# Splitting the first PSUM copy by bank and moving one softmax piece forward in a fused dynamic convolution and feed-forward kernel

## Chip, cores and metric

Each run is one core of one Trainium2 chip. The metric is the device time of one execution in microseconds (us). Ratios are the mean time of one kernel's runs over the mean of the other's runs of the same rounds, so they are not quite the ratios of the medians that are quoted. Executions over 1.5% slower than the fastest of the same kernel are left out of the means. The 95% intervals belong to the ratios.

## The reference

```python
# dynamic convolution: B=8, S=4096, D=192, H=8 heads, K=7 taps
w = exp(weight_gen - max(weight_gen, -1)); w = w / (sum(w, -1) + 1e-9)
x_pad = concat([zeros(B, 6, D), x], axis=1)
out = einsum('bshk,bskhg->bshg', w, unfold(x_pad))    # 7 rows back, per head
# feed-forward: d_ff = 2048
h = maximum(out.reshape(32768, 192) @ w_in, 0)
return (h * h) @ w_out
```

## The kernel before

TensorE does the convolution as matmuls against banded weights (tile `yp` in PSUM), the first feed-forward matmul (`h`) and the second (`o`). ScalarE evacuates `yp` to `y`, makes `t = relu(h)`, the softmax's exp and half of the output evacuation. VectorE squares (`g = t*t`), sums, inverts and scales the softmax (`ssum`, `rcp`, `v`), makes the bands (`bd`) and adds the second half of the output (`o_sb`). A plan of letters orders the work: `u` is a hidden unit (12 matmuls of 256 columns in the first two blocks, 6 of 512 later, then one `t` and one `g`), `M` half of a pair of second matmul groups, `C` the next block's convolution, `E` an exp, `S` a softmax scaling, `B` the bands.

```python
ps_h = tile_pool(bufs=3, PSUM)        # [128, 1024] f32: two banks a tile; h and yp share it
ps_o = tile_pool(bufs=1, PSUM)        # o0, o1: one bank each
...
def st_conv(j):
    th = n * TB // 2                  # 256 columns in blocks 0 and 1, 512 later
    per = 1024 // th                  # chunks of y in one yp tile: 4, later 2
    yps = [ps_h.tile([P, 2 * TB], f32, name="yp") for _ in range(-(-NK // per))]
    ...                               # matmuls into yps
    for n, yp in enumerate(yps):
        k0, k1 = n * per, min((n + 1) * per, NK)          # NK = 3 chunks
        copies = ((k0, k1, nc.scalar.copy),)
        if j == 0:
            copies = ((0, 1, nc.scalar.copy),) + tuple(
                (k, k + 1, nc.vector.tensor_copy) for k in range(1, NK))
        for a, b, copy in copies:
            copy(out=y[:, a:b, 0:th], in_=yp[:, (a - k0) * th : (b - k0) * th] ...)
...
def soft(s):                          # "S": one piece of a part, all on VectorE
    lo, hi = next(s.softs)
    s.total(lo, hi); s.recip(lo, hi); s.scale(lo, hi, nc.vector)
...
steady = "MuMuuu" * 3 + "MuuuMCu"     # blocks from 4 on; E, S and B are filled in by TIMES
3: "L5 L6 M S3 u u u M u u u u M u M B6 E4 u u u M M B7 u u u M u M C S4 u",
TIMES = {(1, 0): ((3, 15), (4, 1)), ...}     # fifth part: scaled before unit 15 of block 3
                                             # and before unit 1 of block 4
```

The softmax here doesn't subtract the row's maximum and nothing guards it: scores larger than these inputs give would overflow.

## Time and profile before

| | before |
|---|---|
| time, median of the first three runs | 748.18 us (747.88 to 750.02) |
| span of the profiled run, granted clock | 746.1 us, 1.000 |
| TensorE busy | 738.3 us (99%) |
| ScalarE, VectorE busy | 624.1 us (84%), 621.9 us (83%) |

TensorE's busy share of 99% says little of its waits: by the page's own legend, matmuls are pipelined and their ends are modelled. The page says where TensorE is *not* the bound: a chain of work that leaves TensorE, and a wait that it has for another engine. There are two such places, the first 25 us and the head of block 4; the prediction shows their lines.

### The profile page before, as it was taken

The page shows a single profiled execution, that of the slowest core. Times are in us where ns is not written, and L with a number is a line of the kernel's source. Part 1 is how long each engine was busy: PE and PEld are TensorE (multiplying, and loading weights), DVE is VectorE, ACT ScalarE, POOL GpSimd, SP SyncE. Part 2 cuts the span into 40 slices and gives each one's busy share as a digit, 9 for nine tenths or more (in the row PEclk, how much of TensorE's full clock was granted, in tenths as well). Part 3 has the DMA queues.
Part 4 walks back from the last instruction along what each step waited for, and adds up shares of the span by engine and source line. Part 5 has one row for each costly group of instructions (what it writes and reads, how often), then busy time and mean ns, then how long its engine had stood idle before and what let it go on. Part 6 is the DMA issues. An engine that isn't in the chain of part 4 may idle for free.

```text
span 746.1 us, 33290 instructions
## 1 busy us (share of the span) xinstructions
PE 738.3 (99%) x15106; PEld 558.0 (75%) x15106; DVE 621.9 (83%) x1003; ACT 624.1 (84%) x755; POOL 88.9 (12%) x130
## 2 busy tenths in 40 slices
PE   8999999999999999999999999999999999999998
PEld 4767777777777797777877777787777777777787
DVE  5999898998889888887889888898888987677853
ACT  5998888898888888888888888888888888888884
POOL 7322220101101100011000110001100011000000
PEclk9999999999999999999999999999999999999999
DMA  8755444435554244643146442265341354442312
GB/s 218 118 100 115 80 93 93 99 71 139 94 118 80 72 59 80 140 83 71 39 78 139 98 69 61 43 139 108 59 80 47 58 108 80 60 73 51 51 45 66
DMA packets 122170, 64.81 MB, mean 87 GB/s; under 512 B 83850, under 2 KB 118637, under 8 KB 121517
## 3 DMA queue, kind: packets, MB, share of 16 engines
q1 hardware_dynamic: 77708, 45.66, 22.3%
q0 software_dynamic: 44176, 16.93, 20.1%
q8 instruction: 118, 1.93, 1.0%
q14 instruction: 24, 0.19, 0.1%
q10 hardware_dynamic: 144, 0.10, 0.0%
HBM read 48.61 MB, written 28.70 MB: 104 GB/s over the span
## 4 chain that ended last, share of the span: by engine, by line
PE 94%; DVE 3%; DMA 1%; ACT 1%; issue 1%; DVEq 0%; ACTq 0%
PE o L482 45%; PE h L448 43%; PE yp L416 6%; DVE bd L348 1%; DVE g L460 1%; DMA wr<-v_first 0%; DMA wg<-in_weight_gen_dram 0%; ACT t L457 0%; DVE v_first L239 0%; DVE ssum L224 0%; DVE rcp L231 0%; ACT ex L217 0%; DVE o_sb L498 0%; ACT y L434 0%; ACT o_sb L496 0%
## 5 line engine op out<-in xcount | busy, mean ns | idle before, releaser
L457 ACT ACTIVATE t<-h 128x1024 f16<-128x1024 f32 x512 | 496.7, 1026 | 64.8 <-PE h L448 64.4
L460 DVE TENSOR_TENSOR g<-t 128x1024 f16<-128x1024 f16 x512 | 333.9, 686 | 99.6 <-ACT t L457 97.0
L482 PEld LDWEIGHTS <-g 64*128 64x128 f16 (+1 forms) x8032 | 351.5, 94 | 55.0 <-issue 4.1
L482 PE MATMUL o<-w_o,g 64*128 64x192 f16 (+1 forms) x8032 | 383.9, 243 | 0.5 <-DVE o_sb L498 0.5
L448 PE MATMUL h<-y,w_i 64*128 64x512 f16 (+1 forms) x3168 | 378.7, 370 | 1.7 <-ACT t L457 0.8
L448 PEld LDWEIGHTS <-w_i 64*128 64x128 f16 x3168 | 163.5, 94 | 114.8 <-issue 5.0
L348 DVE TENSOR_TENSOR bd<-wr,mask 128x4160 f16<-128x4160 f16 (+3 forms) x89 | 149.3, 1701 | 3.7 <-DMA wr<-v_first 3.7
L300 POOL DMA_DIRECT2D xt<-in_x_dram x62 | 51.6, 836 | 443.0 <-PE yp L416 420.1
L496 ACT COPY o_sb<-o 128x384 f32<-128x384 f32 x129 | 62.3, 483 | 33.9 <-PE o L482 33.9
L498 DVE TENSOR_TENSOR o_sb<-o,o_sb 128x384 f32<-128x384 f32 x123 | 68.2, 554 | 8.4 <-ACT o_sb L496 5.6
L434 ACT CAST y<-yp 128x1024 f16<-128x1024 f32 (+1 forms) x64 | 47.7, 796 | 15.0 <-PE yp L416 15.0
L416 PE MATMUL yp<-bd,xt 128*32 128x104 f16 (+8 forms) x3864 | 51.8, 208 | 0.6 <-DVE bd L348 0.3
L416 PEld LDWEIGHTS <-xt 128*32 128x32 f16 (+3 forms) x3864 | 46.1, 91 | 7.0 <-issue 6.4
L217 ACT ACTIVATE ex<-wg 128x448 f32<-128x448 f32 (+2 forms) x44 | 27.2, 618 | 1.9 <-DMA wg<-in_weight_gen_dram 1.9
L239 DVE TENSOR_TENSOR v_big<-ex,rcp 128x112 f16<-128x112 f32 (+1 forms) x136 | 27.3, 263 | 1.6 <-DMA vd<-v_big 0.4
L224 DVE TENSOR_REDUCE ssum<-ex 128x64 f32<-128x448 f32 (+2 forms) x44 | 26.1, 593 | 2.4 <-ACT ex L217 2.4
L231 DVE RECIPROCAL rcp<-ssum 128x64 f32<-128x64 f32 (+2 forms) x44 | 23.7, 539 | 1.5
L290 POOL DMA_DIRECT2D xt<-in_x_dram x7 | 3.8, 548 | 137.2 <-PE yp L416 137.2
L330 POOL DMA_DIRECT2D wr<-v_first x31 | 16.8, 559 | 18.3 <-DVE v_first L239 18.1
L546 PE MATMUL wp<-warm 128*128 128x512 f16 x39 | 10.5, 434 | 1.3 <-DVE warm L538 1.3
L546 PEld LDWEIGHTS <-warm 128*128 128x128 f16 x39 | 4.2, 110 | 6.9 <-issue 2.4
L239 DVE TENSOR_TENSOR v_first<-ex,rcp 128x112 f16<-128x112 f32 (+1 forms) x48 | 9.1, 255 | 0.3
(25 smaller groups left out, 28.6 us busy)
## 6 DMA issues: line engine op xcount, KB each, us to landing
out_dram<-o_sb SPq DMA_DIRECT2D x63, 384.0 KB, 2.9
xt<-in_x_dram POOLq DMA_DIRECT2D x42, 240.0 KB, 5.7
wg<-in_weight_gen_dram SPq DMA_DIRECT2D x4, 1064.0 KB, 8.2
xt<-in_x_dram POOLq DMA_DIRECT2D x20, 192.0 KB, 5.4
wr<-vd SPq DMA_DIRECT2D x38, 80.0 KB, 3.7
vd<-v_big SPq DMA_DIRECT2D x5, 512.0 KB, 5.5
wg<-in_weight_gen_dram SPq DMA_DIRECT2D x5, 392.0 KB
wg<-in_weight_gen_dram SPq DMA_DIRECT2D x3, 616.0 KB, 4.5
```

Source lines behind the costliest of these rows:

```text
L217: nc.scalar.activation(out=self.ex[:, lo:hi].rearrange("p r g k e -> p (r g) k e"), in_=self.wg[:, lo:hi].rearrange("p r (g e) k -> p (r g ...
L239: eng.tensor_tensor(out=bass.AP(tensor=v.tensor, offset=v.offset + lo * H * SL + lo % SL * 2 + g * SL * 2, ap=[list(v.ap[0]), [H * SL + 2, ...
L300: eng.dma_start(out=dst[:, first:last], in_=ap)
L348: nc.vector.tensor_tensor(out=bd_t[j][:, H * lo : H * (lo + len(tiles) * n)].rearrange("p (g m c) -> p g m c", g=shape[1], c=2 * SL), in0= ...
L416: nc.tensor.matmul(out=yps[k // per][p0 : p0 + m, col + a : col + b], lhsT=x_t[s][:, i, 32 * q : 32 * q + m], rhs=bd[:, h // 2, h % 2, a - ...
L434: copy(out=y[:, a:b, 0:th], in_=yp[:, (a - k0) * th : (b - k0) * th].rearrange("p (k c) -> p k c", c=th),)
L448: nc.tensor.matmul(out=h[:, half, jj * th : (jj + 1) * th], lhsT=w_in_chunk(u * per + jj, slot, half), rhs=y_t[j][r0 : r0 + RT, k, 0:th], ...
L457: nc.scalar.activation(out=t1, in_=h, func=ActF.Relu)
L460: nc.vector.tensor_tensor(out=g, in0=t1, in1=t1, op=AluOp.mult)
L482: nc.tensor.matmul(out=oo[:, cc * Dm : (cc + 1) * Dm], lhsT=g[r0 : r0 + n, cc * P : (cc + 1) * P], rhs=w_o[r0 : r0 + n, fc, :], start=(fc ...
L496: nc.scalar.copy(out=o_sb, in_=o[0][:, c])
L498: nc.vector.tensor_tensor(out=o_sb, in0=o[1][:, c], in1=o_sb, op=AluOp.add)
```

## The change

Its intent has two parts. In block 0 three chunks of y are copied out of PSUM before the first hidden matmuls can run in full. Chunks 0 and 1 fill one bank and chunk 2 lies in the next; each engine is to copy one bank, side by side. In block 4 VectorE has two softmax pieces close together ahead of an output addition that TensorE waits for; one of them goes earlier, into idle time, and its exp goes earlier still.

```diff
             if j == 0:
-                copies = ((0, 1, nc.scalar.copy),) + tuple(
-                    (k, k + 1, nc.vector.tensor_copy) for k in range(1, NK)
-                )
+                copies = ((0, 2, nc.scalar.copy), (2, NK, nc.vector.tensor_copy))
@@
-            3: "... M M B7 u u u M u M C S4 u",
+            3: "... M M B7 u u u E4 M u M C S4 u",
@@
-            (1, 0): ((3, 15), (4, 1)),
+            (1, 0): ((3, 15), (4, 0)),
```

## The prediction

> **What bounds the kernel now.** I read the page first, then the table of waits, then the chain of waits in order of time, and last the timelines of the two stretches that the diff touches. The page:
>
> ```profile
> span 746.1 us, 33290 instructions
> PE 738.3 (99%) x15106; PEld 558.0 (75%) x15106; DVE 621.9 (83%) x1003; ACT 624.1 (84%) x755; POOL 88.9 (12%) x130
> PE 94%; DVE 3%; DMA 1%; ACT 1%; issue 1%; DVEq 0%; ACTq 0%
> ...
> L482 PE MATMUL o<-w_o,g 64*128 64x192 f16 (+1 forms) x8032 | 383.9, 243 | 0.5 <-DVE o_sb L498 0.5
> ```
>
> TensorE is busy for 99% of the span and is 94% of the chain that ended last. From 90 to 732 us the table of busy times by stretch gives it 641.90 of 642.00 us, from 25 to 81 us 55.94 of 56.00. A change outside TensorE can therefore gain only where TensorE stands still. The granted clock is 1.000 and there is one core, so no slow die enters. TensorE stands still in two places that matter here: the start, up to about 25 us, and once in the middle, the single wait for the second output addition (0.5 us) in the last line above. The diff touches exactly these two.
>
> The chain at the first y (start, length, what):
>
> ```profile
> 14.63 0.45 PE yp L416 x16
> 15.09 0.02 issue
> 15.11 0.38 ACT y L434
> ...
> 15.86 0.41 DVE y L434
> 16.27 2.27 DVE bd L348 x2
> ```
>
> and the timeline of 14.9 to 20 us:
>
> ```profile
> 15.11 0.37 ACT L434 CAST y<-yp 128x256 f16<-128x256 f32 x1 [1.94 <-PE yp L416]
> 15.51 0.75 DVE L434 CAST y<-yp 128x256 f16<-128x256 f32 x2 [0.93 <-ACT y L434]
> ...
> 15.99 2.91 PE L448 MATMUL h<-y,w_i 64*128 64x256 f16 x47 [0.19 <-DVE y L434]
> ...
> 16.32 2.29 PEld L448 LDWEIGHTS <-w_i 64*128 64x128 f16 x43 [0.22 <-issue]
> 16.97 2.85 ACT L457 ACTIVATE t<-h 128x1024 f16<-128x1024 f32 x3 [1.49 <-PE h L448]
> ```
>
> The reader is to see that VectorE's copies start only at 15.51, when ScalarE's copy is over, although yp was whole at 15.09. The third chunk is ready at 16.27, and the weight loads pause until 16.32. ScalarE's first squaring input, t, follows at 16.97, and from there to 25 us ScalarE is never idle (5.00 of 5.00 us busy from 20 to 25), so this start sets everything up to 25 us.
>
> The second place, VectorE and then TensorE around the head of block 4:
>
> ```profile
> 79.57 0.69 DVE L460 TENSOR_TENSOR g<-t 128x1024 f16<-128x1024 f16 x1 [0.49 <-ACT t L457]
> 81.34 0.69 DVE L460 TENSOR_TENSOR g<-t 128x1024 f16<-128x1024 f16 x1 [1.08 <-ACT t L457]
> 82.11 0.56 DVE L498 TENSOR_TENSOR o_sb<-o,o_sb 128x384 f32<-128x384 f32 x1
> 82.58 0.49 DVE L224 TENSOR_REDUCE ssum<-ex 128x48 f32<-128x336 f32 x1
> ...
> 86.89 1.89 DVE L460 TENSOR_TENSOR g<-t 128x1024 f16<-128x1024 f16 x3
> 88.69 0.55 DVE L498 TENSOR_TENSOR o_sb<-o,o_sb 128x384 f32<-128x384 f32 x1
> ```
>
> ```profile
> 88.57 0.24 PE L482 MATMUL o<-w_o,g 64*128 64x192 f16 x1
> 89.29 1.48 PE L482 MATMUL o<-w_o,g 64*128 64x192 f16 x31 [0.48 <-DVE o_sb L498]
> ```
>
> VectorE has 1.08 us free before 81.34, and then two softmax pieces (the fifth part's second, 82.58 to 84.23, and a piece of the seventh, 84.83 to 86.89) pile up behind 82.11. The addition that empties the output bank ends at 89.24, and TensorE's second matmul into it waits until 89.29.
>
> **What the Trainium skill says.** The page "PSUM — Partial Sum Buffer", Terms, says that a bank is 2 KiB per partition and that two engines must not be on one bank at once, reads included; its Specifications say that ScalarE and VectorE may read in parallel where there is no bank collision. In block 0 a chunk of yp is 256 fp32 columns, so chunks 0 and 1 fill a bank and chunk 2 lies in the next. That agrees with the trace: VectorE's copy of chunk 1 waited 0.93 us for ScalarE's of chunk 0. No run so far shows the two engines reading different banks of one tile together.
>
> "VectorE: DVE Perf Modes", the errata section, gives copies out of PSUM 120 cycles plus the columns at 0.96 GHz on VectorE and 172 plus the columns at 1.2 GHz on ScalarE: for 256 columns 392 and 357 ns. The trace has 418 and 372, for 512 columns on ScalarE 592 (31 copies; 570 by the page). I use the trace's. "ScalarE: Activation LUTs", section on what a table load costs, says that back-to-back activations overlap by about 93 ns: three t in 2.85 us against 1.026 each are a pitch of 0.91, so 0.11 here.
>
> **Part 1, the first y.** Removed: ScalarE's copy of 256 columns (0.372) and one of VectorE's two (0.418). Added: a ScalarE copy of 512 columns (0.592). VectorE keeps chunk 2 alone, on another bank.
> - ScalarE: 15.11 + 0.59 = 15.70, so chunks 0 and 1 come at 15.70 instead of 15.49 and 15.94.
> - VectorE: chunk 2 from about 15.11 to 15.53, instead of 16.27.
> - TensorE: the first hidden matmul goes at 15.74 (0.04 after its release, as now 15.49 to 15.53). It is 0.2 later, but nothing interrupts it: 47 matmuls in 2.91 us are about 0.06 each, and the fifth, the first that needs chunk 2, goes at 15.74 + 4 x 0.06 = 15.98 instead of 16.32. From that fifth to the first t is 16.97 - 16.32 = 0.65, so t starts at 16.63: **0.34 earlier**.
> - VectorE reaches the bands of the second sub-block at about 15.5 instead of 16.19 (their rows landed by 15.0, and the x tile whose landing released GpSimd's gate at 14.56) and the cast of x at 17.8 instead of 18.45, which opens the second convolution before TensorE gets to it. This 0.7 us lies beside ScalarE's chain and is not added.
> - The next thing that ScalarE can meet is the second part's exp, now at 19.70. Its input's last packet landed at 19.09; at 19.70 - 0.34 = 19.36 it is there, with 0.27 to spare. So the shift should reach 25 us, where TensorE becomes the bound (the chain leaves ScalarE at 25.02), and I count 0.32 of the 0.34.
>
> **Part 2, the fifth softmax part.** Nothing is added or removed. One exp of 336 elements (0.525) moves from 79.41 to between the t ending at 74.34 and the one that starts at 74.74 after 0.41 us idle; with the overlap it takes 0.44 and costs at most 0.05. VectorE's last piece of that part moves ahead of the block's first g:
> - It needs 84.23 - 82.58 = 1.65 us. Behind the g of 79.57 (pitch 0.61) it runs from 80.18 to 81.83. The next g goes at 81.83 instead of 81.34, the addition at 82.43 instead of 82.11, ending at 82.99. TensorE needs that bank at 83.34, so no wait appears, with 0.3 to spare.
> - The next g waits for a t that ends at 83.51, so at 83.55; the other softmax piece 84.15 to 86.21 (2.06 as now); three g to 88.01 (1.80 as now); the addition 88.01 to 88.56, instead of 89.24.
> - TensorE's group of 32 now takes 88.57 to 90.55 = 1.98 us; the same group elsewhere takes 1.32 (83.34 to 84.66, 85.31 to 86.63). So the wait costs 0.66, more than the 0.48 that the table of waits shows, since matmuls overlap. With the addition done at 88.56 and the second matmul due at about 88.61, the wait is gone or nearly: **0.60 to 0.66**, counted as 0.62.
>
> **Sum.** 0.32 + 0.62 = 0.94 us, both on the path that sets the end. The rest of TensorE's work is unchanged and follows. From the median of 748.18 this gives 747.24; from the lowest of the three runs 746.9. I say **747.2 us**, about 0.13% less.
>
> **Rivals.**
> - *The two copies stay one after the other* (something other than the bank orders them, such as the shared tile y). For it: the trace never shows two engines on y at once. Against it: the ordered chunks share a bank. Then chunk 2 would come at 16.1, t at about 16.8, and part 1 gives 0.1 to 0.15: 747.4.
> - *A transfer sets the start.* The exp's input landed only 0.27 before it is wanted; if it lands later, ScalarE waits in order and part 1 gives perhaps 0.1, or nothing: 747.4 to 747.6.
> - *The wait in block 4 moves instead of going.* VectorE is full there, my margin at 88.6 is about 0.05 and at 83.34 about 0.3. Some tenths could remain: 747.4 to 747.7.
> - *VectorE's earlier start is worth more.* The second convolution opens 0.7 us earlier; for it, TensorE idles 0.26 before it at 19.16; against it, ScalarE has no idle time there. At best 0.3 more: 746.9.
> - *Nothing is seen.* The three runs before span 747.88 to 750.02, wider than the whole gain.
>
> **Range and chances.** The rivals lie between 746.9 and 748.2, and a median of three wanders by some 0.3 to 0.4 on its own, so the range is 746.5 to 748.2. Two per cent would be 15 us; the stretches touched hold only about 1 us of idle TensorE time between them. Faster by over 2%: 0.01. Within 2%: 0.985. Slower by over 2%: 0.005.
>
> **What would show it.** Right: ScalarE's y copy of 512 columns at about 15.11 and VectorE's of 256 columns beside it; first t near 16.63; VectorE's bands near 15.5; no wait of TensorE for an output addition in the table of waits; the exp of 336 elements near 74.3; a span of about 745.2. Wrong: VectorE's y copy starting only after ScalarE's; the exp still at 19.70; a remaining or new wait of TensorE near 83 or 88 us; or a later wait between 25 and 60 us that takes back the start's gain.

## The result

| | before | changed |
|---|---|---|
| median of four runs | 748.41 us (747.88 to 750.02) | 747.64 us (747.02 to 748.43) |
| ratio, 95% interval | | 0.9987 (0.9968 to 1.0005) |
| span of the profiled run | 746.1 us | 746.6 us |

The median fell by 0.8 us and lies in the predicted range. The *profiled* span is longer, though, and that has to be understood first. The timelines of the first y after the change (start, length, engine, line, operation, out<-in, count, idle time before and what ended it):

```profile
15.76 0.58 ACT L432 CAST y<-yp 128x512 f16<-128x512 f32 x1 [1.94 <-PE yp L416]
17.50 2.86 ACT L455 ACTIVATE t<-h 128x1024 f16<-128x1024 f32 x3 [1.16 <-PE h L446]
...
12.63 2.60 DVE L348 TENSOR_TENSOR bd<-wr,mask 128x832 f16<-128x832 f16 x5 [4.15 <-DMA wr<-v_first]
16.37 0.42 DVE L432 CAST y<-yp 128x256 f16<-128x256 f32 x1 [1.15 <-ACT y L432]
16.71 2.35 DVE L348 TENSOR_TENSOR bd<-wr,mask 128x3328 f16<-128x3328 f16 x2
...
16.39 3.04 PE L446 MATMUL h<-y,w_i 64*128 64x256 f16 x48 [0.67 <-ACT y L432]
```

VectorE's first band product, which waits for a DMA and is not touched by the change, starts at 12.63 instead of 11.98. So this execution began 0.65 us late, and every later time has to be read from a common event. I take ScalarE's first y copy (15.11 before, 15.76 after). From there:

- **The copies are not side by side.** VectorE's starts at 16.37, 0.03 after ScalarE's ended (15.76 + 0.58 = 16.34). The first t comes 1.74 us after the first copy started, before 1.86: a gain of 0.12, not 0.34.
- The hidden matmul at which the chain changes from ScalarE to TensorE (25.06 before) comes 9.85 after the copy, before 9.95: 0.10 of it arrive.

Block 4 after, VectorE and then TensorE:

```profile
80.07 0.69 DVE L458 TENSOR_TENSOR g<-t 128x1024 f16<-128x1024 f16 x1 [0.48 <-ACT t L455]
80.68 0.49 DVE L224 TENSOR_REDUCE ssum<-ex 128x48 f32<-128x336 f32 x1
...
82.93 0.55 DVE L496 TENSOR_TENSOR o_sb<-o,o_sb 128x384 f32<-128x384 f32 x1
...
88.51 0.55 DVE L496 TENSOR_TENSOR o_sb<-o,o_sb 128x384 f32<-128x384 f32 x1
89.04 0.69 DVE L458 TENSOR_TENSOR g<-t 128x1024 f16<-128x1024 f16 x1
89.95 0.69 DVE L458 TENSOR_TENSOR g<-t 128x1024 f16<-128x1024 f16 x1 [0.22 <-ACT t L455]
90.56 2.39 DVE L348 TENSOR_TENSOR bd<-wr,mask 128x832 f16<-128x832 f16 x2
```

```profile
87.13 2.11 PE L446 MATMUL h<-y,w_i 64*128 64x512 f16 x18
89.07 1.52 PE L480 MATMUL o<-w_o,g 64*128 64x192 f16 x32
90.39 0.85 PE L446 MATMUL h<-y,w_i 64*128 64x512 f16 x6
```

The addition ends at 89.06 and TensorE's group runs without a break from 89.07. From the hidden matmul ahead of it to the one behind it take 90.39 - 87.13 = 3.26 us, before 90.55 - 86.63 = 3.92. That is the 0.66 of the prediction. But the chain of waits of the changed kernel goes through VectorE again one pair of groups later:

```profile
94.15 0.48 DVE o_sb L496
94.63 0.04 issue
94.67 1.48 PE o L480 x31
```

A group's second matmul again waits for an addition. Here the table of waits is blind: it has no line for TensorE waiting for `o_sb`, since the gap behind the first matmul's modelled end is only 0.13 us. From matmul to matmul it is 0.37 us where 0.04 is usual. The addition and the group there, first before and then after:

```profile
93.87 0.55 DVE L498 TENSOR_TENSOR o_sb<-o,o_sb 128x384 f32<-128x384 f32 x1
94.46 1.54 PE L482 MATMUL o<-w_o,g 64*128 64x192 f16 x32
...
94.07 0.55 DVE L496 TENSOR_TENSOR o_sb<-o,o_sb 128x384 f32<-128x384 f32 x1
```

The stretch from 90.55 to 95.78 before, 5.23 us, takes 5.53 after. So 0.30 of the 0.66 goes back within 6 us. Sum for the changed kernel: 0.10 + 0.66 - 0.30 = 0.46 us, about half of the 0.94 predicted.

### The profile page after: what moved, and what is told of

It is laid out like the page before. It is cut to its first block, busy times and chain, and to the rows that moved or that the text cites. A ratio compares the mean times of both kernels' runs of the same rounds, so it can differ in the third digit from the quotient of the medians.

```text
span 746.6 us, 33289 instructions
## 1 busy us (share of the span) xinstructions
PE 738.7 (99%) x15106; PEld 556.1 (74%) x15106; DVE 621.7 (83%) x1002; ACT 624.4 (84%) x755; POOL 89.3 (12%) x130
## 4 chain that ended last, share of the span: by engine, by line
PE 91%; DVE 4%; DMA 2%; ACT 2%; issue 1%; DVEq 0%; ACTq 0%; SPq 0%
PE o L480 43%; PE h L446 42%; PE yp L416 6%; DVE bd L348 2%; DVE g L458 1%; ACT t L455 1%; DMA vd<-v_big 1%; DMA wr<-v_first 1%; DMA wg<-in_weight_gen_dram 0%; DVE v_big L239 0%; ACT ex L217 0%; DVE o_sb L496 0%; DVE ssum L224 0%; DVE rcp L231 0%; DVE v_first L239 0%
```

## The experiments

The profiles are compared in five intervals, each between starts of instructions, so that the late begin of an execution does not enter. They end at the 505th of 3168 hidden matmuls; what lies behind is told under e9 and e10. A: first y copy to first t. B: first y copy to the 109th hidden matmul (25.06 in before). C: 415th to 433rd hidden matmul (86.63 to 90.55). D: 433rd to 457th (90.55 to 95.78). E: 475th to 505th (100.71 to 107.92).

| kernel | A | B | C | D | E | median us | ratio to before, 95% interval |
|---|---|---|---|---|---|---|---|
| before | 1.86 | 9.95 | 3.92 | 5.23 | 7.21 | 748.41 | |
| e9, e10: before again | 1.86 | 9.96 | 3.92 | 5.23 | 7.21 | 747.54, 748.75 (one each) | |
| changed | 1.74 | 9.85 | 3.26 | 5.53 | 7.21 | 747.64 | 0.9987 (0.9968 to 1.0005) |
| e6: changed again | 1.74 | 9.93 | 3.26 | 5.54 | 7.21 | 747.90 | 0.9986 (0.9974 to 0.9998) |
| e1, e8: part 1 alone | 1.75 | 9.84 | 3.92 | 5.23 | 7.21 | 748.30 | 0.9993 (0.998 to 1.0007) |
| e2: part 2 alone | 1.86 | 9.95 | 3.26 | 5.54 | 7.21 | 748.17 | 0.9991 (0.9979 to 1.0004) |
| e3: yp in two tiles | 1.50 | 9.59 | 3.26 | 5.54 | 7.21 | 747.21 | 0.998 (0.9966 to 0.9994) |
| e4: bands later | 1.75 | 9.91 | 3.26 | 5.23 | 8.34 | 748.70 | 1.0003 (0.999 to 1.0016) |
| e5: e3, one band product later | 1.50 | 9.63 | 3.26 | 5.23 | 7.21 | 747.90 | 0.9983 (0.9969 to 0.9997) |
| e7: y in two tiles | 1.75 | 9.84 | 3.26 | 5.54 | 7.21 | 747.35 (one) | |

e1 to e4 shared one set of runs of before (median 748.43), e5 and e6 another (748.87); medians of different sets are not to be compared. The line of e1 and e8 has e8's intervals and e1's time. A single profile repeats an interval to 0.02 (B of the changed kernel only to 0.08, see e6), while a time of a few runs is uncertain by 0.1 to 0.2%; the reasons are therefore read from the intervals.

**e1 and e8, part 1 alone.** The diff's first hunk only.

> Only the copies of the first y are changed; the softmax order is that of before. Theory S (the two copies stay one after the other, because both read the one tile yp): VectorE's y copy again starts only when ScalarE's of 512 columns ends, from the start of ScalarE's y copy to the first t 1.74 us (before: 1.86; after: 1.74), so about 0.1 gained at the start, and the wait of TensorE for the output addition near 89 us stays at 0.5 us. Rival, my recorded step (the copies overlap): 1.52 us. Time against before: 0.1 less under S, 0.3 less under the recorded step.

> The kernel of e1 again, whose only profile fell in a slow execution (952.5 us, granted clock 0.754) and cannot be compared. 1.74 us from the start of ScalarE's first y copy to the first t, and TensorE's wait near 89 us as before (0.72 from matmul to matmul).

e1's one profile fell in an execution of 954.33 us with a granted clock of 0.754; its other four runs were fast. So it was profiled again as e8: A is 1.75 and C stays 3.92, as theory S expected. The recorded step is out: part 1 gives 0.11 in A and in B, and nothing in block 4. In this one profile even that is gone by the 415th hidden matmul: from the 109th to it are 61.71 us, against 61.51 to 61.62 in all the others.

**e2, part 2 alone.** The other two hunks only.

> Only the softmax order is changed; the copies are those of before. Theory G (given back): TensorE's wait near 89 us is gone (0.65 us gained on the matmuls after it against before), but a new wait for the addition of the next output pair appears near 94.5 us, because the bands of the next block stand before that addition on VectorE, and takes about 0.3 of it back, net 0.35. Rival, my recorded step: no new wait, net 0.62. From the start of ScalarE's first y copy to the first t: 1.86 as before. Time against before: 0.35 less under G.

A and B are as before, C is 0.66 shorter, D 0.31 longer. Part 2 gives 0.35 net. The parts are independent of each other: C and D are the same with part 1 (the changed kernel) and without.

**e3, yp in two tiles.** In block 0 yp has 256-column chunks, four to a tile. With two to a tile, chunk 2 gets a tile of its own; the banks that are read stay one for each engine.

```diff
-        per = 1024 // th
+        per = 2 if j == 0 else 1024 // th
@@
-                copies = ((0, 2, nc.scalar.copy), (2, NK, nc.vector.tensor_copy))
+                copies = ((k0, k1, (nc.scalar.copy, nc.vector.tensor_copy)[n]),)
```

> The changed kernel with the first yp in two PSUM tiles: ScalarE copies the one with chunks 0 and 1, VectorE the one with chunk 2. The result is unchanged. Theory S (the shared tile yp orders the copies in the program): VectorE's y copy now starts within 0.1 us of ScalarE's, and from the start of ScalarE's y copy to the first t it is 1.50 to 1.55 us instead of 1.74. Rival H (the two engines disturb each other when they read PSUM, or the tile y orders them): the copies are still apart, or overlap but take clearly longer than 0.58 and 0.42, and the interval stays at about 1.74. Time against the changed kernel: 0.2 less under S, the same under H.

The timelines of e3:

```profile
15.36 0.59 ACT L432 CAST y<-yp 128x512 f16<-128x512 f32 x1 [1.87 <-PE yp L416]
16.86 2.85 ACT L455 ACTIVATE t<-h 128x1024 f16<-128x1024 f32 x3 [0.92 <-PE h L446]
...
15.42 0.42 DVE L432 CAST y<-yp 128x256 f16<-128x256 f32 x1 [0.55 <-PE yp L416]
```

VectorE's copy now waits for TensorE and starts 0.06 after ScalarE's. Side by side they take 0.59 and 0.42, what each takes alone. A is 1.50, the prediction's 1.52 (16.63 - 15.11) to 0.02, and B falls by 0.36 against before. The semaphores in the traces say the same: in the changed kernel VectorE's copy waits on the one that ScalarE's copy counts up, in e3 on the one that ScalarE's copy itself waits on, which TensorE counts up. So the order was put in when the program was made, for the tile that both engines read, although they read different banks of it. Contention of the two engines (rival H) is out.

**e7, y in two tiles.** The other tile that the copies share, as a control: chunk 2 of the first y goes to a tile of its own, and the hidden matmuls read it there (left out here); yp stays whole.

```diff
+        if j == 0:
+            y_last.append(const.tile([P, 1, TB], f16, name="y_last"))
@@
-                    out=y[:, a:b, 0:th],
+                    out=(y_last[0][:, :, 0:th] if j == 0 and a == 2 else y[:, a:b, 0:th]),
```

> The changed kernel with chunk 2 of the first y in an SBUF tile of its own, yp left whole: the other tile that the two copies share. Theory S (yp orders them): VectorE's copy still starts only behind ScalarE's, 1.74 us from the start of ScalarE's copy to the first t. Rival (y orders them): the copies overlap, 1.50 us as in e3. No time is asked.

```profile
14.48 0.59 ACT L436 CAST y<-yp 128x512 f16<-128x512 f32 x1 [1.78 <-PE yp L420]
...
15.10 0.42 DVE L436 CAST y_last<-yp 128x256 f16<-128x256 f32 x1 [1.15 <-ACT y L436]
```

Nothing changes: the copy still waits for ScalarE. With e3, where y is shared and the copies overlap, the tile yp alone makes the order in the changed kernel.

**e4, bands later.** The new wait near 94.5 follows 2.39 us of band products on VectorE. They were put behind the addition that comes late.

```diff
-            us = {4: (7, 9), 6: (7, 9)}.get(...)
+            us = {4: (9, 10), 6: (7, 9)}.get(...)
```

> The changed kernel with the next block's bands in block 4 moved from before the 8th and 10th hidden units to before the 10th and 11th, so behind the output addition at 94.1. Theory G: TensorE's new wait of 0.3 to 0.45 us near 94.5 is gone and the matmuls behind it are 0.3 us earlier against the changed kernel, unless a later addition is now late. Rival: VectorE is simply full in block 4, the wait appears again at the next addition (near 101 us), and nothing is gained. Time against the changed kernel: 0.3 less under G, the same under the rival.

The wait near 94.5 is gone (D is 5.23 again), but E grows from 7.21 to 8.34, so my theory's expectation of a gain failed and the rival written beside it came true. VectorE and TensorE of e4:

```profile
88.97 0.69 DVE L458 TENSOR_TENSOR g<-t 128x1024 f16<-128x1024 f16 x1 [0.22 <-ACT t L455]
89.88 0.69 DVE L458 TENSOR_TENSOR g<-t 128x1024 f16<-128x1024 f16 x1 [0.22 <-ACT t L455]
91.35 0.69 DVE L458 TENSOR_TENSOR g<-t 128x1024 f16<-128x1024 f16 x1 [0.77 <-ACT t L455]
...
100.74 0.55 DVE L496 TENSOR_TENSOR o_sb<-o,o_sb 128x384 f32<-128x384 f32 x1
```

```profile
101.34 1.48 PE L480 MATMUL o<-w_o,g 64*128 64x192 f16 x31 [0.88 <-DVE o_sb L496]
```

Without the bands VectorE idles 0.22 + 0.22 + 0.77 = 1.21 us between 88 and 92, because the next t is not there yet, and the work that was deferred then makes the addition near 101 late. VectorE has nearly no time free between 84 and 101 us. A deferral must not be larger than the slack of the addition behind it.

**e5, one band product later.** On top of e3, only the 832-column product (0.58 us) goes behind the addition near 94. The changed kernel's next addition ended at 100.42 + 0.55 = 100.97 and its bank was wanted at 101.51, so there was 0.5 to spare. The diff is shortened and its comments are added.

```diff
-                at(j, u, "B", a + n)
+                if (j, n) == (4, 1):
+                    at(j, u, "A", a)                             # tile 0 of the first bands
+                at(j, u, "D" if (j, n) == (4, 0) else "B", a + n)  # D: B without tile 0
```

> The kernel of e3 with one of block 4's band products (832 columns, 0.58 us on VectorE, a pitch of about 0.5) moved from before the output addition near 94 us to behind it. Theory F (VectorE is full from 84 to 101 us, the next addition has 0.4 to 0.5 us to spare): the addition near 94 comes 0.5 earlier, TensorE's wait there (0.37 from matmul to matmul in e3) is gone, the matmuls behind it are 0.31 earlier against e3, and no wait comes near 101. Rival, as in e4: the wait turns up at the addition near 101. Time against before: e3 had 747.21 against 748.43; 0.3 less than e3 under F, the same under the rival.

```profile
92.77 0.55 DVE L496 TENSOR_TENSOR o_sb<-o,o_sb 128x384 f32<-128x384 f32 x1
93.23 2.85 DVE L348 TENSOR_TENSOR bd<-wr,mask 128x832 f16<-128x832 f16 x3
```

The addition ends at 93.32, TensorE's group starts at 93.50 and takes its usual 1.32 to the next hidden matmul. C, D and E are 3.26, 5.23 and 7.21 together for the first time, as theory F expected. Against before the sum is 0.32 (B) + 0.66 (C) = 0.98 us: these intervals are what the prediction had described. The kernel beats the kernel before (interval 0.9969 to 0.9997); its median equals that of the changed kernel in the same set (747.90 both), and 0.5 us between these two is below what six runs resolve. Nor do the times show the 0.3 that was expected against e3 (ratios 0.9983 and 0.998).

**e6, the changed kernel again.**

> The changed kernel again, unaltered, for a time beside e5 on the same chip and a second profile. From the start of ScalarE's first y copy to the first t 1.74 us, VectorE's copy behind ScalarE's, no wait near 89 us, a wait of 0.37 from matmul to matmul near 94.5. If the start up to the first band product (12.63 us in the first profile, 11.98 in that of before) is set by when the first loads land, and not by the change, it differs from the first profile's. Time: 0.5 us less than before (0.1 from the start, 0.35 from block 4).

C and D repeat to 0.01, and the first band product starts at 11.48 instead of 12.63, so the 0.65 of the first profile was not the change. A is 1.74 again, but B is 9.93: of 0.12 only 0.02 reach TensorE. ScalarE's chain in e6 shows where they go:

```profile
16.36 2.80 ACT t L455 x3
19.15 0.04 issue
19.20 0.94 ACT ex L217
```

The exp of the second part starts 2.84 after the first t, in the changed kernel's first profile 2.73 (20.23 - 17.50). The last packet of its input landed at 19.09 in e6 and the exp started 0.11 later; the same distance is seen in e3 (19.50, 19.61), e4 (19.14, 19.24) and e5 (19.36, 19.46). In the first profile of the changed kernel the packet landed at 19.65, 0.58 ahead of the exp. In such executions the load now sets the exp, and a start that is still earlier would gain nothing unless the load is issued sooner; that was not tried.

**e9 and e10, before again.**

> The kernel before, unaltered, for a second profile of it. In the profiles of the changed kernels TensorE has two to five gaps of 0.25 to 0.94 us between 190 and 715 us that end no wait, at much the same places; the only profile of before has one. If they are chance (instruction supply or the like), this profile has two to five as well. If the change brings them, it has one. From the start of ScalarE's first y copy to the first t 1.86 us, a wait of 0.72 from matmul to matmul near 89 us, no wait near 94.5.

> The same once more, a third profile of before, with the same expectation: two to five gaps without a wait between 190 and 715 us if they are chance, one if the change brings them; 1.86 us from the first y copy to the first t. The first band product starts somewhere between 11.3 and 12.7 us, as in the other profiles, if the landing of the first loads varies from run to run.

All five intervals repeat. The first band product starts at 11.47 and 12.70, so the begin varies by more than the whole effect of the change. TensorE has gaps without a wait at 192 and 712 us in e9 and at 260, 554 and 622 us in e10, of 0.28 to 0.43 us from one matmul's start to the next. Such gaps are thus not new with the change. From 120 us on, the eleven profiles (all but e1's slow one) have one to seven each, 38 in all, the largest 0.94 us (e5, at 621). None of these matmuls has a wait in the program. The DMA packets in the traces narrow the cause: in all 38, the matmul behind the gap starts 1.24 to 1.55 us after the end of the last packet of the queue that the page calls "instruction" (q8: 118 packets of 16 KB, one about every 6 us); of all matmuls from 120 us on in the kernel before, 4.5% start at that distance. So TensorE seems to wait there for its next instructions. That is read from the traces and not tested, and why some packets come late is open.

What lies behind interval E is not equal either. From the 505th hidden matmul to the last, the three profiles of before take 624.22 to 624.39 us and the eight others 624.59 to 625.63. From the first y copy to the last hidden matmul there are 717.02 to 717.23 us before, 716.89 and 717.12 in the changed kernel and 717.29 in e5. So the profiles show the gain up to the 505th hidden matmul, and do not show that all of it reaches the end. Whether the longer rest is chance or is brought by the changes is open. That something arrives rests on the times alone: the intervals of e3, e5 and e6 lie below 1, but barely.

## Why the prediction was right or wrong

**The time** was right: 747.64 lies in the range of 746.5 to 748.2, and "within 2%" held. The fall of the medians, 0.8, is near the predicted 0.94, but the intervals account for only 0.37 to 0.46 of it; the rest cannot be told from the scatter of runs, which is about as large. That the number came so close is luck: two steps of it failed, and they took half of the gain away.

**Part 1, VectorE's copy.** The failed step is "VectorE: chunk 2 from about 15.11 to 15.53". It rested on the reading that the bank orders the copies. The changed kernel, e3 and e7 show that a shared tile is enough: two banks of one tile were still read in order. In the kernel before, the ordered copies share the bank and the tile, and no run parts the two there. The 0.93 us that the prediction gives as VectorE's wait for ScalarE is all of its idle time; yp was whole only at 15.09, so the wait for ScalarE is at most 15.51 - 15.09 = 0.42. What remains is ScalarE's longer copy in place of a copy and a VectorE copy: 0.12 in A, as the first rival had it ("0.1 to 0.15", though it suspected the tile y, which e7 rules out), and 0.02 to 0.11 at TensorE. The argument against that rival, that the ordered chunks share a bank, explained nothing, because both readings expect the same wait there.

**Part 1, everything behind the copy** was right: where the copies do overlap, A is 1.50 against 1.52, and 0.32 to 0.36 reach TensorE against the 0.32 counted. The second rival, the transfer, was right in part: the exp's input does set the exp in four of the profiles, at a cost of up to 0.1. The fourth, that VectorE's earlier start is worth more, did not show: in e3 B falls by 0.36, no more than A.

**Part 2, the head of block 4** was right in all its steps up to this group. The moved piece starts at 80.68, 0.61 after the g of 80.07; the addition behind it ends at 83.48, TensorE starts at 83.84, no wait; the wait near 89 is gone, 0.66. The exp cost TensorE nothing: up to 86.63 the interval from B's end is no longer than before.

**Part 2, "The rest of TensorE's work is unchanged and follows"** failed. I stopped reading one addition too early. Before, the next addition ended at 93.87 + 0.55 = 94.42 and TensorE's group started at 94.46: it had no slack, only no visible wait. Counted from the hidden matmul ahead of the change (86.63 and 87.13), TensorE wants that bank 0.66 earlier (7.83 before, 7.17 after), but VectorE delivers only 0.30 earlier (the addition starts 7.24 after it before, 6.94 after), because the g at 89.95 waits for a t whose hidden matmuls did not move. The difference is what D gives back. The third rival said that tenths could remain, but at the same addition; e2, e4 and e5 show it at the next. Whether the work behind the 505th hidden matmul follows unchanged is not shown either (see e9 and e10).

## What to carry to other kernels

A semaphore wait between two copies says who was waited for, not which shared thing made the program put the order in: look for a case that separates the candidates, or change one of them. When a wait of the bounding engine is removed, check the slack of the next few hand-overs as well, from the matmul starts and not from listed waits, since an engine that was just in time before becomes late by what the other gained. Work may be deferred only by as much as the next hand-over has to spare.

## What the Trainium skill lacked or had wrong

- "PSUM — Partial Sum Buffer", Specifications: that ScalarE and VectorE read different banks in parallel is right (e3: 0.59 and 0.42 us, 0.06 apart, no longer than alone). It doesn't say that a program may still order two engines' reads of one PSUM tile in different banks: 0.03 us between the end of one copy and the start of the other in the changed kernel, and two tiles remove it. No page that I read has this.
- "VectorE: DVE Perf Modes", the errata section: copies out of PSUM took 418 ns on VectorE for 256 columns (392 by its row), 372 and 592 ns on ScalarE for 256 and 512 (357 and 570): 15 to 26 ns more.
- "Perfetto Trace Analysis", Optimization Strategy, looks for gaps between slices on the bounding engine. Here the loss from start to start was 0.66 us where the gap between slices was 0.48, and a loss of 0.30 showed no gap that was listed.
- "Runtime: NRT & Kernel Launch", Instruction fetch mechanics, lacks how long an engine stands when a block of instructions comes late. TensorE's 38 gaps of 0.25 to 0.94 us without a wait each ended 1.24 to 1.55 us after a packet of the "instruction" queue.
